# Attention and a mixture of experts on one core: where block one's last stores are issued, and where the first sums of w2 stand

## The chip, the cores and the metric

The kernel runs on one core of one Trainium2 chip. The metric is the device time of one execution in microseconds (us), the median of several runs. The core has five engines that work on their own: TensorE (PE, matrix multiplication), VectorE (DVE), ScalarE (ACT), GpSimd (POOL) and SyncE (SP), which here only issues DMAs. Each engine takes its instructions in the order in which the program wrote them, so an instruction that waits holds up all that stand behind it on that engine. That holds for the DMA issues too: those of SP stand in one line, and those of GpSimd stand in line with its arithmetic.

## The reference

```
attention (4 batches, 8 heads, 576 positions, width 64, 128 features):
  phi(x) = exp(x omT - |x|^2/2 - rowmax) / sqrt(128)
  out = (phi(q) (phi(k)^T v)) / (phi(q) sum(phi(k)) + 1e-6)
x = out as rows: 2304 x 512
mixture (4 experts, hidden width 1024):
  p = probs / (sum(probs) + 1e-9)
  y = sum over e of p[:, e] * (relu(x @ w1[e]) @ w2[e])
```

All is float32. The kernel reaches that precision with three matrix products for one: each operand is split into a high part (rounded to the matrix type) and a low part (what is left), and high*high, high*low and low*high are summed.

## The kernel before, in words

The mixture is done in 27 visits. A visit takes one half of one expert's hidden width (four chunks of 128) and one block of rows: visits 0 to 10 take block zero, 11 to 18 block one (768 rows, 6 output tiles of 128), 19 to 26 block two (1024 rows, 8 tiles). Visits of block one and two are in `fast` (L827). The first layer there is a seven-product scheme on quarter blocks (Strassen's), for two groups g of hidden chunks: `p1`, `p2`, `p5`, `p6`, `p7`, `p3`, `p4` are its products, each six matmuls of 512 columns in block two (L866). A product either opens a PSUM bank ("u", "b2", "b5") or, with start=False, adds onto one whose old contents were taken out before: `keep` (L870) copies a bank to SBUF on ScalarE, `both` (L876) adds a bank to such a copy on VectorE, after which ScalarE makes the relu's high part `hh` (L887) and VectorE its low part `hl` (L891). So p7(0) and p4(0) can start only when the bank "u" was read: p7(0) after the copy that p6(0) makes, p4(0) after the add that follows p7(0).

Visits of block two (`DEEP`, L475) use the same scheme for the second layer as well (`sevens`, L943), and for that they need sums of blocks of w2. The generator `w2_sides` (L540) makes them in steps: `sums_of(f)` is four tensor_tensor of 128x256 on GpSimd (L551 to L554) that read two loaded chunks of w2; `summed` splits half of such a sum (ScalarE copies the high part, GpSimd subtracts: line L498 and L501, tile w2s); `plain(c)` splits a chunk itself the same way (w2h, w2l); and a `load("w2")` behind plain(0), plain(2) and the second sums_of issues the load of a chunk on SP when a buffer is free (tile w2r, three buffers). For visit 19 the order of its steps is: sums 0, two splits of them, plain 0 with the load of its last chunk (called load (19,3) below), plain 1, plain 2 with a load, plain 3, sums 1 with two loads, two splits. `start_sides2` (L817) does the first step, `on_sides2` (L823) one further step, `prepare` (L848) as many as the list `steps2` says. At the head of visit 19 two steps are taken (L840), then one behind p1(0), one behind p5(0), one behind sum2(0), p2(1) and p7(0) each.

The split first layer of a block-two visit is not made again: `keep_sides` (L599) wrote it to DRAM in block one (eight DMAs on SP, `kept`), and `fetched` (L639) brings it back with eight DMAs that GpSimd issues (w1ah, w1al, w1sh, w1sl for two groups), two for each `next(ready)`. They wait until the buffers that they fill are free.

The output tiles of a visit: `outputs` (L684) multiplies, `gather` (L701) adds the result to the tile's accumulator on VectorE (L718), `gathered` (L725) counts; in the last visit of a block the finished accumulator is put on the list `stores`, and `store(keep)` (L733) issues stores on SP until `keep` are left. In visit 18 VectorE also makes the operands of block two between the gathers, steps of `build(2)` (L778): the differences `less` (L790) and the low parts xbl (L501) of seven 128x1024 tiles, two steps a tile.

Of the kernel before, what the change touches and what calls it, by code (L numbers as in the profile page):

```python
# [14 lines left out]
def attention_moe(ctx, tc, kT, qT, kd, qd, kn, qn, vn, omT, probs, w1, w2, out):  # L15
# [15 lines left out]
    E, FP, P, _ = w1.shape  # L31
# [34 lines left out]
    def bank(name):  # L66
        return psum.tile([P, 512], F32, tag="ps", name=name)
# [396 lines left out]
    def visit(u, n, c0, m):  # L464
        return (u, *HALVES[n], c0, m)

    BIG = {1: (START, 6 * P), 2: (START + 6 * P, 8 * P)}
    visits = [visit(0, n, 0, 2 * P) for n in range(3)]
# [6 lines left out]
    DEEP = range(N0 + NV, len(visits))  # L475
# [56 lines left out]
    def split_w2():  # L532
        if not later_w2:
            return
        v, c = later_w2.pop(0)
        W[v, "w2", c] = a, b = pair_of(("w2h", 512), ("w2l", 512))
        split(raw.pop((v, "w2", c)), a, b, nc.scalar, nc.gpsimd)
        load("w2")
# [145 lines left out]
    def outputs(v, hs, ps, t, cs):  # L684

        ts_ = slice(t * P, (t + 1) * P)
        for c in cs:
            (ha, hc), (wa, wc) = hs[c], W[v, "w2", c]
            nc.tensor.matmul(ps, ha[:, ts_], wa, start=(c == 0), stop=False)  # L689
            nc.tensor.matmul(ps, ha[:, ts_], wc, start=False, stop=False)  # L690
            nc.tensor.matmul(ps, hc[:, ts_], wa, start=False, stop=(c == FH - 1))  # L691
# [9 lines left out]
    def gather(v, ps, t, cs=slice(0, DM)):  # L701
        _, e, _, c0, n = visits[v]
        i = c0 // P + t
        sc = pr[:, i, e:e + 1]
        if i not in acc:
            if v in DEEP and t == 3:
                acc[i] = [att.tile([P, H], F32, tag=x, name="acc", bufs=1) for x in ("kvh", "kvl")]
            else:
                acc[i] = held([P, DM], "acc", F32)
        to = part(i, cs)  # L710
        fresh = [h for h in (0, H) if cs.start <= h < cs.stop and (i, h) not in begun_at]
        begun_at.update((i, h) for h in fresh)
        if fresh and v in DEEP:
            nc.vector.tensor_scalar(to, ps, sc, None, ALU.mult)
        elif fresh:
            nc.scalar.activation(to, ps, AF.Copy, scale=sc)
        else:
            nc.vector.scalar_tensor_tensor(to, ps, sc, to, ALU.mult, ALU.add)  # L718
# [6 lines left out]
    def gathered(v, t):  # L725
        i = visits[v][3] // P + t
        n = visits[v][4]
        n_tiles[i] += 1
        if n_tiles[i] == NV and v + 1 < len(visits):
            stores.append((i, acc.pop(i)))  # L730
        store(1 if v + 1 < len(visits) and t + 1 < n // P else 0)

    def store(keep):  # L733
        while len(stores) > keep:
            i, t = stores.pop(0)
            nc.sync.dma_start(out[i * P:(i + 1) * P], t)

    def plain(v):
# [18 lines left out]
        for t in range(tiles):  # L757
            ps = bank("g2")
            outputs(v, hs, ps, t, range(2))
            if v == N0 - 2 and t in (0, 2):  # L760
                next(building)
            if last:
                next(building, None)
            yield 0.5
            outputs(v, hs, ps, t, range(2, FH))
            gather(v, ps, t)
            gathered(v, t)
            for _ in range(FH // tiles):
                split_w()
            next(ready, None)  # L770
            if last:
                next(building, None)
            yield 0.5
# [43 lines left out]
    def start_sides2(v):  # L817
        B = {}
        g = w2_sides(v, B)
        next(g)  # L820
        sides2[v] = B, g

    def on_sides2(v):  # L823
        if v in sides2:
            next(sides2[v][1])

    def fast(v):  # L827

        u, _, _, _, n = visits[v]
        tiles, n = n // P, n // 2  # L830
# [3 lines left out]
        ready = sides(v + 1) if v + 1 < len(visits) else iter(())  # L834
# [13 lines left out]
        def prepare():  # L848
            if deep:
                for _ in range(steps2.pop(0)):  # L850
                    next(ready2, None)
            else:
                split_w2()
# [4 lines left out]
        def product(g, p, where, start=True):  # L858
            if start:
                P_[g][where] = bank("g1")[:, :n]  # L860
            ps = P_[g][where]
            (wa, wc), (xa, xc) = W[v, "w1", g][p], X[p]
            for k in range(2):
                w = slice(k * P, (k + 1) * P)
                for a, x, at in ((wa, xa, 0), (wa, xc, 1), (wc, xa, 2)):
                    nc.tensor.matmul(  # L866
                        ps, a[:, w], x[:, k], start=(start and k + at == 0), stop=(k == 1 and at == 2), skip_group_check=not start
                    )

        def keep(g, where, name):  # L870
            P_[g][name] = t = held([P, 512], "sum", F32)[:, :n]
            nc.scalar.activation(t, P_[g][where], AF.Copy)  # L872
# [23 lines left out]
        def p1(g):  # L896
            product(g, 1, "u")
            keep(g, "u", "p1")
# [4 lines left out]
        def sum2(g):  # L903
            both(g, 0, 0, "b2", "p1", hold=g == 1)
# [5 lines left out]
        def p6(g):  # L910
            product(g, 6, "u", start=False)
            keep(g, "u", "u2")
# [19 lines left out]
        def begun(t):  # L932
            g2[t] = bank("g2")
            outputs(v, hs, g2[t], t, range(2))
# [8 lines left out]
        def sevens():  # L943
# [87 lines left out]
            for t in range(tiles):  # L1031
                gathered(v, t)
# [10 lines left out]
        p6(0)  # L1043
        if deep:
            prepare()
        p1(1)
        sum2(0)
        if deep:
# [16 lines left out]
        if deep:  # L1065
# [6 lines left out]
            yield from sevens()  # L1072
            return
        prepare()
        p6(1)
        next(ready, None)
        begun(0)
        p7(1)
        begun(1)
# [5 lines left out]
        for t in range(tiles):  # L1085
            if t in g2:
                outputs(v, hs, g2[t], t, range(2, FH))
            else:
                g2[t] = bank("g2")
                outputs(v, hs, g2[t], t, range(FH))  # L1090
            gather(v, g2[t], t)
            gathered(v, t)
            next(ready, None)
            for _ in range(2 if t < 4 else 1):
                next(more, None)
            if v + 1 == DEEP[0] and t == 1:
                start_sides2(v + 1)
            elif t > 2:
                on_sides2(v + 1) if t < 5 else None
            yield 1  # L1100
        for _ in more:
            pass
# [205 lines left out]
    def emit():  # L1308
        pairs, g1 = begin()
        later = [Halves(b, hp) for b in range(1, B) for hp in range(NP)]  # L1310
        windows = {
            0: (first_rest(pairs, opening(later[0])), 15 / 11),
            3: (later_ticks(later[:-NP], True), 76 / 45.4),
            N0: (chain(opening(later[-NP]), later_ticks(later[-NP:], False)), 54 / (NV * (BIG[1][1] // P + 1) * 0.8)),
        }
        ticks, n, done, per = iter(()), 0, 0.0, 0
        for v in range(len(visits)):
            if v in windows:
                for _ in ticks:
                    pass  # L1320
                ticks, per = windows[v]
                n, done = 0, 0.0
            for share in first_visit(g1) if v == 0 else fast(v) if v >= N0 else plain(v):
                done += share
                while n < done * per:
                    next(ticks, None)
                    n += 1
        store(0)
# [61 lines left out]
```

## Time and profile before

| | us |
|---|---|
| runs timed: median (lowest to highest of 3) | 899.49 (898.46 to 899.87) |
| the profiled execution: time | 898.98 |
| its span, first to last instruction | 897.2 |
| busy: PE, VectorE, ScalarE, GpSimd | 884.8, 596.9, 468.3, 564.0 |
| mean granted clock of TensorE, share of full speed | 0.996 |

The span is the time from the first to the last instruction of the profiled execution; the time has about 2 us around it. All places given below as times, such as 584.08, are us from the start of the span. A timeline row has start, duration, engine, line, operation, what it writes and reads, shapes and how many; in brackets the time for which the engine sat idle before it and what ended that. Matmuls overlap, so a matmul's duration is longer than the step from one start to the next.

### The profile page before, as it was taken

The numbers are of one execution on the slowest core, as the hardware profiler recorded it, in microseconds if no ns is written. First come the engines' busy times: TensorE is split into PE (matmuls) and PEld (weight loads), VectorE is DVE, ScalarE is ACT, GpSimd is POOL, SyncE is SP. The second block draws the span as 40 slices with busy tenths as digits, with TensorE's granted clock in tenths as the row PEclk, the third lists the DMA queues.
The fourth block names the chain that finished last, engine by engine and source line by source line (L and its number), as shares of the span: only waits on it lengthen the run. The fifth ranks groups of instructions, "written<-read, shape, count | busy, mean of one in ns | idle before, by whom it ended". The sixth has DMA issues, their size and how long they took to land.

```text
span 897.2 us, 14825 instructions
## 1 busy us (share of the span) xinstructions
PE 884.8 (99%) x5484; PEld 789.6 (88%) x5484; DVE 596.9 (67%) x1026; ACT 468.3 (52%) x1038; POOL 564.0 (63%) x494
## 2 busy tenths in 40 slices
PE   9999999999999999999999999799999999999998
PEld 9988888889888898988988989589889898998988
DVE  6764567666778547577676676865858485675847
ACT  5555676776774565464555536244443434344442
POOL 6656464655645454435444345589898988989874
PEclk9999999999999999999999999999999999999999
DMA  7564454444521855545455255724151443415132
GB/s 184 171 221 118 136 161 146 153 135 151 168 71 47 314 173 209 214 136 189 174 194 212 71 188 214 256 58 154 59 176 54 159 135 112 154 59 176 43 135 94
DMA packets 64552, 134.01 MB, mean 149 GB/s; under 512 B 10624, under 2 KB 21056, under 8 KB 64480
## 3 DMA queue, kind: packets, MB, share of 16 engines
q1 hardware_dynamic: 54512, 102.95, 35.0%
q0 software_dynamic: 9360, 29.82, 10.0%
q8 instruction: 43, 0.70, 0.3%
q10 hardware_dynamic: 608, 0.30, 0.1%
q14 instruction: 29, 0.24, 0.1%
HBM read 98.96 MB, written 34.08 MB: 148 GB/s over the span
## 4 chain that ended last, share of the span: by engine, by line
PE 86%; DVE 8%; issue 2%; ACT 2%; DMA 1%; POOL 1%; SPq 0%; POOLq 0%; ACTq 0%; DVEq 0%
PE g L866 25%; PE g L941 17%; PE g L689 7%; PE g L691 7%; PE g L690 7%; PE g L674 3%; PE g L676 3%; PE g L675 3%; PE kv L314 2%; DVE xbl L501 2%; PE k_ps L266 1%; PE q_ps L266 1%; DMA kept<-w1ah 1%; PE qt_ps L325 1%; PE k_ps L147 1%
## 5 line engine op out<-in xcount | busy, mean ns | idle before, releaser
L501 POOL TENSOR_TENSOR w2l<-w2r,w2h 128x512 fp32r<-128x512 f32 x93 | 120.9, 1305 | 91.2 <-ACT w2h L498 77.7
L718 DVE SCALAR_TENSOR_TENSOR acc<-g,pr,acc 128x256 f32<-128x256 f32 (+1 forms) x278 | 139.3, 541 | 31.9 <-PE g L691 21.9
L501 POOL TENSOR_TENSOR w1sl<-w1r,w1sh 128x512 fp32r<-128x512 f32 (+1 forms) x43 | 75.2, 1749 | 70.8 <-ACT w1sh L498 54.7
L689 PE MATMUL g<-w2h,hh 128*128 128x512 f32 x280 | 112.7, 402 | 0.4 <-ACT kp L296 0.2
L691 PE MATMUL g<-w2h,hl 128*128 128x512 f32 x280 | 109.8, 392 | 0.0
L690 PE MATMUL g<-w2l,hh 128*128 128x512 f32 x280 | 109.6, 391 | 0.0
L891 DVE SCALAR_TENSOR_TENSOR hl<-sum,hh 128x384 fp32r<-128x384 f32 (+1 forms) x64 | 45.2, 709 | 85.6 <-ACT hh L887 55.8
L878 DVE TENSOR_TENSOR sum<-g,sum 128x384 f32<-128x384 f32 (+1 forms) x96 | 59.4, 620 | 64.3 <-PE g L866 57.1
L866 PE MATMUL g<-xbh,w1sh 128*128 128x384 f32 (+1 forms) x256 | 93.9, 367 | 5.5 <-ACT sum L872 5.5
L866 PE MATMUL g<-xbl,w1sh 128*128 128x384 f32 (+1 forms) x256 | 93.5, 365 | 1.1 <-DVE xbl L501 1.1
L866 PE MATMUL g<-xbh,w1sl 128*128 128x384 f32 (+1 forms) x256 | 93.1, 363 | 0.0
L501 POOL TENSOR_TENSOR w1al<-w1r,w1ah 128x512 fp32r<-128x512 f32 (+1 forms) x45 | 51.5, 1159 | 51.6 <-ACT w1ah L498 38.8
L872 ACT ACTIVATE sum<-g 128x384 f32<-128x384 f32 (+1 forms) x96 | 50.3, 540 | 50.2 <-PE g L866 49.3
L498 ACT ACTIVATE w2h<-w2r 128x512 fp32r<-128x512 f32 x90 | 55.0, 627 | 38.8 <-DMA w2r<-in_w 33.2
L866 PE MATMUL g<-xbh,w1ah 128*128 128x384 f32 (+1 forms) x192 | 70.1, 365 | 0.0
L866 PE MATMUL g<-xbl,w1ah 128*128 128x384 f32 (+1 forms) x192 | 69.6, 362 | 0.0
L866 PE MATMUL g<-xbh,w1al 128*128 128x384 f32 (+1 forms) x192 | 69.5, 362 | 0.0
L691 PEld LDWEIGHTS g<-w2h,hl 128*128 128x128 f32 x280 | 52.5, 188 | 11.9 <-DVE hl L924 0.4
L689 PEld LDWEIGHTS g<-w2h,hh 128*128 128x128 f32 x280 | 52.7, 188 | 11.2 <-DVE sum L878 0.7
L690 PEld LDWEIGHTS g<-w2l,hh 128*128 128x128 f32 x280 | 52.7, 188 | 8.6
L866 PEld LDWEIGHTS g<-xbh,w1sh 128*128 128x128 f32 x256 | 48.5, 189 | 11.8 <-ACT sum L872 6.0
L887 ACT ACTIVATE hh<-sum 128x384 fp32r<-128x384 f32 (+1 forms) x64 | 35.1, 551 | 41.5 <-DVE sum L878 41.0
(212 smaller groups left out, 2442.3 us busy)
## 6 DMA issues: line engine op xcount, KB each, us to landing
w2r<-in_w SPq DMA_DIRECT2D x108, 256.0 KB, 2.9
w1r<-in_w SPq DMA_DIRECT2D x38, 512.0 KB, 3.6
kept<-w1sh SPq DMA_DIRECT2D x16, 512.0 KB, 4.8
kept<-w1sl SPq DMA_DIRECT2D x16, 512.0 KB, 5.3
w1sh<-kept POOLq DMA_DIRECT2D x16, 512.0 KB, 6.1
w1sl<-kept POOLq DMA_DIRECT2D x16, 512.0 KB, 6.8
kept<-w1ah SPq DMA_DIRECT2D x16, 384.0 KB, 4.3
kept<-w1al SPq DMA_DIRECT2D x16, 384.0 KB, 4.4
```

Of the source, the lines that this page charges most:

```text
L498: hi.activation(a, t, AF.Copy)
L501: lo.tensor_tensor(c, t, f32(a), ALU.subtract)
L689: nc.tensor.matmul(ps, ha[:, ts_], wa, start=(c == 0), stop=False)
L690: nc.tensor.matmul(ps, ha[:, ts_], wc, start=False, stop=False)
L691: nc.tensor.matmul(ps, hc[:, ts_], wa, start=False, stop=(c == FH - 1))
L718: nc.vector.scalar_tensor_tensor(to, ps, sc, to, ALU.mult, ALU.add)
L866: nc.tensor.matmul(ps, a[:, w], x[:, k], start=(start and k + at == 0), stop=(k == 1 and at == 2), skip_group_check=not start)
L872: nc.scalar.activation(t, P_[g][where], AF.Copy)
L878: nc.vector.tensor_tensor(t, P_[g][where], t, ALU.add)
L887: nc.scalar.activation(ha, t, AF.Relu)
L891: nc.vector.scalar_tensor_tensor(x, y, 0.0, f32(z), ALU.max, ALU.subtract)
L941: nc.tensor.matmul(to, x, w, start=(start and f + k == 0), stop=(f + k == 3), skip_group_check=not start)
```

## The change

Three edits, all at the border between visit 18 and visit 19.

1. `gathered` issues no stores in visit 18; the six stores of block one are issued in visit 19, behind p6(0).
2. The first step of visit 19's `w2_sides` (the four sums) is taken in visit 18 ahead of p6(1) instead of behind output tile 1, and the `next(ready)` that stood behind p6(1), with two of GpSimd's load issues, is left out there, so that each of the four pairs of issues comes one output tile later.
3. The two splits of these sums come in output tiles 0 and 1, ahead of that tile's load issues, instead of tiles 3 and 4.

```diff
@@ gathered
-        store(1 if v + 1 < len(visits) and t + 1 < n // P else 0)
+        if v + 1 != DEEP[0]:
+            store(1 if v + 1 < len(visits) and t + 1 < n // P else 0)
@@ fast
         p6(0)
         if deep:
             prepare()
+            if v == DEEP[0]:
+                store(0)
         p1(1)
@@
         prepare()
+        if v + 1 == DEEP[0]:
+            start_sides2(v + 1)
         p6(1)
-        next(ready, None)
+        if v + 1 != DEEP[0]:
+            next(ready, None)
         begun(0)
@@
             gathered(v, t)
+            if t < 2:
+                on_sides2(v + 1)
             next(ready, None)
             for _ in range(2 if t < 4 else 1):
                 next(more, None)
-            if v + 1 == DEEP[0] and t == 1:
-                start_sides2(v + 1)
-            elif t > 2:
-                on_sides2(v + 1) if t < 5 else None
             yield 1
```

## Rows read from the trace of the kernel before

**Rows 1.** The page, its part 1: busy time of each engine.

```profile
PE 884.8 (99%) x5484; PEld 789.6 (88%) x5484; DVE 596.9 (67%) x1026; ACT 468.3 (52%) x1038; POOL 564.0 (63%) x494
```

**Rows 2.** Waits of TensorE, whole span: us in total, times, longest.

```profile
PE g L866 <- ACT sum L872: 5.5, 1, 5.5
```

**Rows 3.** The chain that ended last, around 580: start, us, what.

```profile
579.02 0.67 DVE acc L718
...
579.71 0.33 SPq L736
...
580.14 2.69 DMA w2r<-in_w
...
583.45 0.59 ACT sum L872
```

**Rows 4.** Timeline of TensorE from 568 to 593.

```profile
568.76 0.39 PE L866 MATMUL g<-xbh,w1ah 128*128 128x512 f32 x1
...
572.84 0.39 PE L866 MATMUL g<-xbh,w1sh 128*128 128x512 f32 x1
574.36 0.50 PE L866 MATMUL g<-xbl,w1sh 128*128 128x512 f32 x1 [1.12 <-DVE xbl L501]
...
578.16 0.39 PE L866 MATMUL g<-xbh,w1al 128*128 128x512 f32 x1
584.08 0.80 PE L866 MATMUL g<-xbh,w1sh 128*128 128x512 f32 x1 [5.53 <-ACT sum L872]
...
589.83 0.39 PE L866 MATMUL g<-xbh,w1ah 128*128 128x512 f32 x1
...
592.55 0.28 PE L941 MATMUL g<-w2h,hh 128*128 128x256 f32 x1
```

**Rows 5.** Stretches: length, busy PE, PEld, DVE, ACT, POOL, granted clock, DMA, GB/s.

```profile
584.10:588.00 3.90, 3.90 (x11) 3.10 (x12) 2.24 (x3) 2.51 (x5) 3.74 (x5) 0.58 0.00 0
```

**Rows 6.** Timeline of VectorE from 555 to 589.

```profile
555.91 0.55 DVE L924 SCALAR_TENSOR_TENSOR hl<-g,hh 128x384 fp32r<-128x384 f32 x1
...
561.68 1.22 DVE L501 TENSOR_TENSOR xbl<-raw_x,xbh 128x1024 fp32r<-128x1024 f32 x1
...
565.16 1.79 DVE L501 TENSOR_TENSOR xbl<-t_k,xbh 128x1024 fp32r<-128x1024 f32 x1
566.88 7.43 DVE L501 TENSOR_TENSOR xbl<-t_q,xbh 128x1024 fp32r<-128x1024 f32 x1
...
579.61 0.68 DVE L878 TENSOR_TENSOR sum<-g,sum 128x512 f32<-128x512 f32 x1
585.06 1.08 DVE L891 SCALAR_TENSOR_TENSOR hl<-sum,hh 128x512 fp32r<-128x512 f32 x1 [4.78 <-ACT hh L887]
...
588.04 0.68 DVE L878 TENSOR_TENSOR sum<-g,sum 128x512 f32<-128x512 f32 x1
```

**Rows 7.** Timeline of GpSimd from 552 to 574.

```profile
552.64 0.59 POOL L642 DMA_DIRECT2D w1ah<-kept  x1 [1.88 <-DMA kept<-w1ah]
...
560.98 0.76 POOL L551 TENSOR_TENSOR va<-w2r 128x256 f32<-128x256 f32 x1
...
563.57 1.60 POOL L553 TENSOR_TENSOR va<-w2r,va 128x256 f32<-128x256 f32 x1
...
566.92 2.56 POOL L501 TENSOR_TENSOR w2s<-va,w2s 128x512 fp32r<-128x512 f32 x2
569.44 3.77 POOL L501 TENSOR_TENSOR w2l<-w2r,w2h 128x512 fp32r<-128x512 f32 x3
```

**Rows 8.** Timeline of SP's DMA issues from 544 to 580.

```profile
544.50 4.12 SPq L494 DMA_DIRECT2D w2r<-in_w  x3
...
558.86 21.18 SPq L736 DMA_DIRECT2D out<-acc  x6
```

**Rows 9.** DMAs issued from 557 to 558: KB each, us to landing.

```profile
w1ah<-kept POOLq DMA_DIRECT2D x1, 384.0 KB, 10.1
w2r<-in_w SPq DMA_DIRECT2D x1, 256.0 KB, 9.9
```

## The prediction

> **What bounds the kernel now.** The page first: TensorE is busy 99% of the span [rows 1], so 12.4 us (897.2 less 884.8) is all that its waits can give back, and matmuls that run slowly come on top. Then TensorE's waits, of which the longest by far is one of 5.5 us on ScalarE's copy of a bank [rows 2]. TensorE's timeline at the head of visit 19 [rows 4] has it ahead of p7(0) at 584.08, and a shorter one, 1.1 on VectorE, in p6(0) at 574.36. The chain [rows 3] tells what is behind the long one, read upwards from 583.45: ScalarE's copy that p7(0) needs stood behind the split plain(3), whose chunk landed 2.69 us after SP issued it at 580.14; SP was at the sixth store until then, and that store waited for the last gather (579.02 to 579.69). The issue rows agree: the stores hold SP from 558.86 to 580.04 [rows 8]. The gather was late because VectorE was: one xbl took 7.43 us from 566.88, where another took 1.22 [rows 6], and it ended at 574.31, 1.1 us after GpSimd had come to the end (573.21) of five splits without a gap [rows 7]. That xbl is what p6(0) waited for too.
>
> What the two waits cost TensorE. Three products, 18 matmuls, step from 568.76 to 572.84: 0.2267 us each. The 36 matmuls of p1(0), p2(0), p5(0), p6(0), p1(1), p2(1) would end at 568.76 + 36 x 0.2267 = 576.92; they ended at 578.16 + 0.23 = 578.39 [rows 4]: 1.47 lost. From there to 584.08: 5.69 lost. The 30 matmuls of p7(0), p5(1), p3(0), p4(0), p6(1) took 584.08 to 592.55, 8.47 for 6.80: 1.67 lost, because the granted clock was 0.58 after the wait [rows 5], that is the lower level of 1.2 GHz for most of that stretch. Sum 8.83 us. After the wait of 1.1 us the clock did not suffer: the 17 matmuls from 574.36 to 578.39 took 4.03 for 3.85.
>
> **The change part by part.**
> *Stores behind p6(0).* SP now comes to load (19,3) as soon as its buffer is free, which is behind GpSimd's part of plain(0). That split ended at 570.7 (first of the three from 569.44, [rows 7]) and can't come much earlier, because its target is read by visit 18's last output tile, which ends at 568.76 [rows 4]. Issued at 569 to 570.7 and landing 2.7 later [rows 3], the chunk is there at 571.7 to 573.4. ScalarE wants it behind its copy of p5(0), whose matmuls end at 572.84 + 0.2: no wait. The copy of p6(0) is then done by about 575.5, and p7(0) starts when TensorE gets to it: 576.92. The six stores issue back to back at some 0.33 us each on an idle queue when the gathers are done; behind them on SP stand only the two loads of sums 1, for visit 20, whose sums come behind the split of T1, over 10 us later. Cost of that: 0. The accumulators are written again only by gathers that stand behind p7(1), p3(1), p4(1) and 48 matmuls of the second layer after L941's first (592.55 before), so nothing waits for the stores.
>
> *Sums ahead of p6(1).* The chunks they read are the second and third of three loads issued from 544.50 to 548.6 [rows 8], and GpSimd stood idle for 1.88 us before 552.64 [rows 7]. So the sums start about 551.3, 2.7 behind the last issue. They took 4.9 us at 560.98 to 565.9 against VectorE's xbl (1.60 for the third, 0.76 for the first, [rows 7]); I take 3.5 to 5. What they may hold up is VectorE in visit 18's p3(1) and p4(1): its last low part ends at 556.46 [rows 6]. The matmul that reads it is the 12th behind p4(1), and p4(1) ends 60 matmuls ahead of 568.76, at 555.16; so it is due at 555.16 + 11 x 0.2267 = 557.65, 1.2 later. If VectorE were kept out for all four sums, that is up to 4.9 less 1.2 = 3.7 us; if it goes in between, as in rows 7 beside xbl, nothing. I take 0: VectorE's instructions there are 0.55 long with idle time between. A gain isn't excluded here, it is counted below (VectorE's xbl).
>
> *Splits in tiles 0 and 1, load issues a tile later.* ScalarE gets to the first split behind the relu whose low part VectorE makes at 555.91 [rows 6], so GpSimd splits at about 556.4, and the first pair of fetches, at 552.64 before, is issued at 557.7; the second split at 558.8, the last pair of fetches by about 563.5 (before: up to 566.9, where the first split begins [rows 7]). p1(0) reads the first pair at 568.76, 11 us later; the slowest fetch took 10.1 [rows 9], while fetches, `kept` writes and stores were all in flight; now the stores are not. p5(0) reads the second pair at 571.5 (issued about 560.7), p1(1) the third at 574.2. Cost 0, with 1 us of cover by the slowest row and 4 or more by a quieter queue.
>
> *VectorE's xbl.* GpSimd now has, while VectorE works through its 16 instructions from visit 18's first gather to the add behind p2(0) (579.61 + 0.68 = 580.29, [rows 6]), two lone splits at 556.4 and 558.8, and plain(0) and plain(1) together, then plain(2) and plain(3) one by one, each behind a ScalarE copy. The excess before was 6.2 in the long xbl, 0.6 in the one ahead of it, and an estimated 0.4 in the difference ahead of that, 7.2. So the add ends between 573.1 (no excess) and 580.3 (the same). Six splits of 1.28 make 7.7 at most; I take two thirds, 5.1: the add ends at 578.2.
>
> The Trainium skill (SBUF — State Buffer, Who interferes with whom, and the section SBUF: two separate sides) has it that a VectorE instruction with two SBUF inputs and a GpSimd instruction that reads SBUF lock each other out, and that the one that starts first holds the port for its whole instruction. Read so, an xbl would wait out one split, not five, and 7.43 should have been about 2.5; rows 6 and 7 show otherwise for splits without a gap. By the rule the add would end at about 577 and the time would be near 890.5.
>
> *The new wait.* p4(0) adds onto the bank "u" that VectorE reads behind p7(0). From the add behind p2(0) VectorE and ScalarE need: relu 0.65, then from the hl at 585.06 to the end of the third add at 588.72 [rows 6] 3.66: together 4.3. Before, this was covered, since p4(0) came at 589.83. Now TensorE is ready for p4(0) at 576.92 + 18 x 0.2267 = 581.0, and the bank at 578.2 + 4.3 = 582.5 plus 0.1 for the hand-over. TensorE waits 1.6.
>
> **Sum.** 8.83 less 1.6 is 7.2. On the profiled execution's time: 898.98 - 7.2 = 891.8 us. That execution is 0.5 under the median of the runs shown (899.49), from which the same sum gives 892.3; both are within one another's spread.
>
> **The rivals.**
> - *VectorE is on time.* The add ends by 576.7, p4(0) waits for nothing: 898.98 - 8.83 = 890.2. For it: GpSimd has only two splits in a row now. Against: six splits fall into VectorE's work, and three lost turns of 1.28 on top of 573.1 make it late.
> - *VectorE is held as long as before.* If sums 1, now directly behind plain(3), keep it out again, the add ends at 580.3 or a little later; p4(0) waits 3.7 or more, with matmuls at the lower clock behind it (up to 1.67): 8.83 - 3.7 - 0 to 1.7 is 3.4 to 5.1, so 893.9 to 895.6. For it: the 7.43 row. Against: sums left VectorE its turn in rows 7.
> - *The load is late anyway, so the change doesn't do what it says.* Load (19,3) now shares the DMA engines with the last fetches, and the load issued among them took 9.9 [rows 9]. Then the chunk lands at 579 to 580.6, p7(0) starts at 580.2 to 581.8 instead of 576.9: 3.3 to 4.9 lost, and up to 1.67 to the clock. 892.3 to 896.7, say 894.5. Against: the fetches are issued by 563.5, six us before.
> - *Slower: the first fetches come too late.* The place is p1(0) at 568.76. It needs the sums, the split and two issues to go before on GpSimd. With the slowest load (9.9) ahead of the sums and the slowest fetch (10.1) behind, the sums start at 558.2, the pair is issued at about 563.8 and 564.9 and lands by 575; the second pair lands about 577.6, and TensorE is at 592.55 - 1 to 3, still not later than before. It decides when the second pair lands past 580.5, 12 us after p1(0)'s place less the 3 us of p1(0) and p2(0): then nothing of the 8.83 is left, and a clock drop puts it at 900 to 904. The fetches would have to take 13 us or more, which no row shows.
>
> **How the numbers follow.** Forecast 0.47 (891.8, by itself 890.6 to 893.4); VectorE on time 0.25; held as before 0.13; load late 0.07; sums in the way of visit 18's relus, 0 to 3.7 us off the forecast, 0.03 (893 to 895.5); slower 0.05. The range goes from 889.9, the whole 8.83 and 0.3 for the spread between runs, to 895.5, and leaves out the slower case and the far ends of two others. A time within 0.2% of before (1.8 us) can't be told from no change by these runs. Faster 0.93, same 0.03 (897.7 to 901.3: the ends of the two late cases and the near end of the slower one), slower 0.04.
>
> **What would show it.** In the profile after: SP's load of w2r at 569 to 571 and the six stores together at 574 to 580; no DMA on the chain around 580; TensorE's 5.5 us wait on ScalarE's sum gone, and in its place a wait of p4(0) on VectorE's sum (L878) of 1 to 2 us; granted clock 1.00 in all stretches of visit 19; GpSimd's sums at 551 to 556 and first fetch at 557 to 558; L941 begun at 584 to 586 instead of 592.55, and everything behind it shifted by the same amount. I am wrong if p1(0) waits for a fetch, if p7(0) still waits for ScalarE, or if what is gained at L941 is lost again later in visits 19 or 20.

## The result and the profile after

The changed kernel takes 891.5 us (median of 4 runs, 889.17 to 892.62); the kernel before, in runs beside it, 899.68. The ratio is 0.9905, 95% interval 0.9878 to 0.9932: faster by about 8 us, 0.9%. Run again later it took 891.49 (6 runs; ratio 0.9910, 0.9894 to 0.9925). Forecast were 891.8 and a range from 889.9 to 895.5, so the number was right. Its make-up was not quite: the border between the two visits gave back all of the 8.8 us, not 7.2, as the rival with VectorE on time had it.

TensorE's waits over the whole span of the profiled execution (total us, times, longest); this answers to [rows 2]:

```profile
PE warm L1120 <- DVE om_r L1111: 1.1, 1, 1.1
PE k_ps L147 <- DVE om L82: 0.8, 1, 0.8
PE g L942 <- DVE hl L925: 0.7, 2, 0.5
PE g L689 <- ACT kp L296: 0.2, 1, 0.2
```

The wait of 5.5 us and the one of 1.1 on xbl are gone, and none has come in their place: the two longest are at the start of the program. TensorE's timeline at the head of visit 19, first matmuls of p1(0), p4(0) and the second layer (lines have moved by one), answers to [rows 4]:

```profile
570.97 0.39 PE L867 MATMUL g<-xbh,w1ah 128*128 128x512 f32 x1
...
583.21 0.40 PE L867 MATMUL g<-xbh,w1ah 128*128 128x512 f32 x1
...
585.94 0.28 PE L942 MATMUL g<-w2h,hh 128*128 128x256 f32 x1
```

From p1(0) to the second layer are 585.94 - 570.97 = 14.97 us for 66 matmuls, 0.2268 each; before it was 592.55 - 568.76 = 23.79 [rows 4]. That is 8.82 gained in this stretch. The granted clock in it was 1.00 (window row: length, busy PE, PEld, DVE, ACT, POOL, clock, DMA, GB/s), where [rows 5] had 0.58:

```profile
570.97:585.94 14.97, 14.97 (x68) 12.38 (x66) 12.41 (x14) 7.72 (x14) 12.67 (x10) 1.00 0.68 231
```

SP's issues, answering to [rows 8]:

```profile
571.61 0.33 SPq L494 DMA_DIRECT2D w2r<-in_w  x1
```

```profile
576.50 3.68 SPq L737 DMA_DIRECT2D out<-acc  x6
```

Load (19,3) goes out at 571.61, 0.6 after p1(0) began, instead of 11.4 after, and lands 3.8 later; the six stores hold SP for 3.7 us instead of 21.2. VectorE and GpSimd, answering to [rows 6, 7]:

```profile
571.01 3.89 DVE L501 TENSOR_TENSOR xbl<-raw_x,xbh 128x1024 fp32r<-128x1024 f32 x2
574.83 0.74 DVE L718 SCALAR_TENSOR_TENSOR acc<-g,pr,acc 128x512 f32<-128x512 f32 x1
575.49 1.65 DVE L501 TENSOR_TENSOR xbl<-raw_x,xbh 128x1024 fp32r<-128x1024 f32 x1
577.06 0.74 DVE L718 SCALAR_TENSOR_TENSOR acc<-g,pr,acc 128x512 f32<-128x512 f32 x1
577.72 0.68 DVE L879 TENSOR_TENSOR sum<-g,sum 128x512 f32<-128x512 f32 x1
...
582.27 0.68 DVE L879 TENSOR_TENSOR sum<-g,sum 128x512 f32<-128x512 f32 x1
```

```profile
560.90 0.59 POOL L642 DMA_DIRECT2D w1ah<-kept  x1
...
569.84 6.21 POOL L501 TENSOR_TENSOR w2l<-w2r,w2h 128x512 fp32r<-128x512 f32 x3 [2.47 <-ACT w2h L498]
```

No xbl takes 7.43 any more; two side by side take 3.89. Three of GpSimd's splits take 6.21, where three took 3.77 before [rows 7]: now GpSimd loses turns too. The add behind p2(0) ends at 578.40, 7.4 after p1(0) began, against 11.5 before; the add that p4(0) needs ends at 582.95, and p4(0) starts at 583.21, just when the 54 matmuls ahead of it are through (570.97 + 54 x 0.2268 = 583.22). Its margin is 0.26 us, and 0.26 in the repeat too (584.29 and 584.55). The first fetch went out at 560.90, 10.1 ahead of p1(0), and nothing waited for it. How long the first pair took to land (KB, us from issue to landing):

```profile
w1ah<-kept POOLq DMA_DIRECT2D x1, 384.0 KB, 5.6
w1al<-kept POOLq DMA_DIRECT2D x1, 384.0 KB, 6.0
```

So w1ah was there at 566.5 and w1al at 567.5, some 4.4 and 3.9 us ahead of the matmuls that read them (570.97 and 571.42).

Behind this stretch nothing changed: from the second layer's first matmul to the last matmul of the kernel are 301.04 us before and 301.28 after. Ahead of it this execution was 2.2 us late, and that has nothing to do with the change. 2.07 of the 2.21 are there at TensorE's first L266 matmul, in the attention, some 470 us ahead of the first edited step (before, then after):

```profile
82.11 1.16 PE L266 MATMUL k_ps<-om_r,k 64*128 64x128 f32 x16
```

```profile
84.18 1.16 PE L266 MATMUL k_ps<-om_r,k 64*128 64x128 f32 x16
```

8.82 less 2.21 less 0.24 is 6.4, the difference of the two spans (897.2 and 890.8).

### The profile page after: what moved, and what is told of

Read it like the earlier page. It is cut to its first block, busy times and chain, and to the rows that moved or that the text cites. A ratio compares the mean times of both kernels' runs of the same rounds, so it can differ in the third digit from the quotient of the medians.

```text
span 890.8 us, 14823 instructions
## 1 busy us (share of the span) xinstructions
PE 884.1 (99%) x5484; PEld 789.4 (89%) x5484; DVE 593.8 (67%) x1026; ACT 468.9 (53%) x1038; POOL 566.3 (64%) x494
## 4 chain that ended last, share of the span: by engine, by line
PE 90%; DVE 4%; issue 2%; DMA 2%; ACT 1%; POOL 1%; SPq 0%; POOLq 0%; ACTq 0%; DVEq 0%
PE g L867 26%; PE g L942 17%; PE g L689 8%; PE g L691 7%; PE g L690 7%; PE g L674 3%; PE g L676 3%; PE g L675 3%; PE kv L314 2%; PE q_ps L266 1%; PE k_ps L266 1%; DMA kept<-w1ah 1%; PE qt_ps L325 1%; PE k_ps L147 1%; PE q_ps L147 1%
## 5 line engine op out<-in xcount | busy, mean ns | idle before, releaser
L501 POOL TENSOR_TENSOR w2l<-w2r,w2h 128x512 fp32r<-128x512 f32 x93 | 123.9, 1337 | 81.6 <-ACT w2h L498 69.8
```

What stands on the lines that cost most here:

```text
L501: lo.tensor_tensor(c, t, f32(a), ALU.subtract)
```

## The experiments

All stretches below run from p1(0)'s first matmul to the first of the second layer in visit 19, in each kernel's profiled execution; without any wait it is 14.97. "Lost to the clock" is the time of the matmuls behind a wait, up to the end of the stretch, less 0.2268 for each. Each ratio is to runs of the kernel before made beside that kernel: their medians were 899.68 for "changed", 899.95 for "changed again", the two halves and the first "splits in tiles 3, 4", and 899.6 for the rest.

| kernel | stretch | wait at | lost to the clock | median us (runs) | ratio, interval |
|---|---|---|---|---|---|
| before | 23.79 | p6(0) 1.47 in all, p7(0) 5.7 | 1.7 | 899.6 (25) | |
| changed | 14.97 | none | 0 | 891.5 (4) | 0.9905, 0.9878 to 0.9932 |
| changed again | 15.02 | none | 0 | 891.49 (6) | 0.9910, 0.9894 to 0.9925 |
| stores only | 21.28 | p6(0) 1.7 in all, p4(0) 2.9 | 1.7 | 897.01 (8) | 0.9968, 0.9955 to 0.9981 |
| sums and splits only | 19.92 | p7(0) 3.2 | 1.75 | 895.23 (6) | 0.9951, 0.9935 to 0.9968 |
| splits in tiles 3, 4 | 17.21 | p4(0) 2.1 | 0.1 | 891.76 (5) | 0.9907, 0.9892 to 0.9923 |
| the same again | 15.61 | p4(0) 0.5 | 0.1 | 892.98 (6) | 0.9931, 0.9908 to 0.9954 |
| VectorE two more | 20.67 | p4(0) 3.1 | 2.6 | 895.74 (6) | 0.9958, 0.9938 to 0.9978 |
| VectorE five more | 24.69 | p4(0) 8.2 | 1.6 | 901.03 (10) | 1.0011, 0.9997 to 1.0025 |
| fetches late | 18.10 (23.89 from where p1(0) is due) | p1(0) 5.8 | 3.1, a second wait in it | 899.82 (10) | 1.0003, 0.9988 to 1.0018 |

**Stores alone** (edit 1 on the kernel before).

```diff
 gathered:
-        store(1 if v + 1 < len(visits) and t + 1 < n // P else 0)
+        if v + 1 != DEEP[0]:
+            store(1 if v + 1 < len(visits) and t + 1 < n // P else 0)
 fast, behind p6(0) and prepare():
+            if v == DEEP[0]:
+                store(0)
```

> The kernel before with edit 1 alone: the six stores behind p6(0) of visit 19, sums and splits where they were. Theory A (two causes: SP's stores ahead of load (19,3), and GpSimd's five splits in a row that keep VectorE's xbl out): the 5.5 us wait of p7(0) goes, the 1.1 us wait of p6(0) on xbl stays, and p4(0) now waits for VectorE about 2.3 us, because the add behind p2(0) still ends 11.5 us after p1(0) begins, as before. From p1(0)'s first matmul to the first of L942: 23.8 - 8.8 + 1.5 + 2.3 = 18.8 us; time about 895. Theory B (the stores alone are the whole gain): 15.0 to 16.4 us, time 890 to 892.

Measured: stretch 21.28, 897.01 us, 2.9 below the runs of before beside it (899.95). TensorE's rows show which waits remain:

```profile
574.62 0.50 PE L867 MATMUL g<-xbl,w1sh 128*128 128x512 f32 x1 [1.34 <-DVE xbl L501]
...
585.64 0.53 PE L867 MATMUL g<-xbh,w1ah 128*128 128x512 f32 x1 [2.75 <-DVE sum L879]
...
590.09 0.28 PE L942 MATMUL g<-w2h,hh 128*128 128x256 f32 x1
```

The wait of p7(0) is gone, that of p6(0) stays, and p4(0) waits for VectorE, as theory A had it; B (the stores are the whole gain) is out. A's size was short by 2.5 us (21.28 for 18.8), for two reasons, and the time, expected at about 895, came out 2 us above. VectorE's and GpSimd's rows:

```profile
567.14 7.43 DVE L501 TENSOR_TENSOR xbl<-t_q,xbh 128x1024 fp32r<-128x1024 f32 x1
574.49 0.74 DVE L718 SCALAR_TENSOR_TENSOR acc<-g,pr,acc 128x512 f32<-128x512 f32 x1
575.15 3.40 DVE L501 TENSOR_TENSOR xbl<-raw_x,xbh 128x1024 fp32r<-128x1024 f32 x2
```

```profile
575.74 1.73 POOL L551 TENSOR_TENSOR w2f<-w2r 128x256 f32<-128x256 f32 x1
577.54 1.60 POOL L552 TENSOR_TENSOR w2f<-w2f,w2r 128x256 f32<-128x256 f32 x1
```

The xbl is 7.43 us long to the hundredth again. The second reason is the clock, below; the first is VectorE. Now that the load is early, the second sums of w2 follow at once and meet VectorE's last xbl (two in 3.40, sums of 1.73 and 1.60 where 0.74 is usual), so the add behind p2(0) ends 12.8 after p1(0), not 11.5. And the wait of 2.75 was followed by the lower clock:

```profile
585.60:589.50 3.90, 3.86 (x10) 3.06 (x11) 2.29 (x3) 1.26 (x3) 1.81 (x2) 0.56 0.00 0
```

**Sums and splits alone** (edits 2 and 3 on the kernel before).

```diff
 the changed kernel, with edit 1 taken out:
-        if v + 1 != DEEP[0]:
+        if True:
             store(1 if v + 1 < len(visits) and t + 1 < n // P else 0)
 ...
-            if v == DEEP[0]:
-                store(0)
```

> The kernel before with edits 2 and 3 alone: sums and splits early, the stores of block one in visit 18 as before. Theory A: xbl is no longer long, the last gather ends about 6.8 us after p1(0) begins instead of 10.9, the sixth store lets SP go 0.4 later, load (19,3) lands 2.7 after that, and p7(0), due 8.2 after p1(0), starts near 11.3 after a wait of 3 us on ScalarE; then 0 to 1.7 us are lost to the clock. From p1(0) to the second layer 18 to 19.7 us, time 894 to 896. Theory B (stores are the whole gain): as before, 23.8 us and 899.5.

Measured: stretch 19.92 and 895.23 us, 4.7 below before, in A's range (its stretch 0.2 above). VectorE was on time (the gather that the sixth store waits for ended 6.8 after p1(0) began), but SP still issued the load behind that store, and ScalarE's split of the chunk, with the copy that p7(0) needs behind it, waited for the DMA; the rows are VectorE's last gather, ScalarE's and TensorE's:

```profile
574.13 0.74 DVE L718 SCALAR_TENSOR_TENSOR acc<-g,pr,acc 128x512 f32<-128x512 f32 x1
```

```profile
578.26 0.63 ACT L498 ACTIVATE w2h<-w2r 128x512 fp32r<-128x512 f32 x1 [5.26 <-DMA w2r<-in_w]
```

```profile
579.43 0.51 PE L867 MATMUL g<-xbh,w1sh 128*128 128x512 f32 x1 [3.05 <-ACT sum L873]
```

So each half of the change leaves the other cause standing. By the stretches the halves give 2.5 and 3.9 alone and 8.8 together: each alone turns part of its gain into a wait that the other would remove, and both of those waits cost a clock drop on top.

**Splits in tiles 3 and 4** (edit 3 undone), run twice.

```diff
             gathered(v, t)
-            if t < 2:
-                on_sides2(v + 1)
             next(ready, None)
             for _ in range(2 if t < 4 else 1):
                 next(more, None)
+            if 2 < t < 5:
+                on_sides2(v + 1)
             yield 1
```

> The changed kernel with edit 3 undone: stores late, sums ahead of p6(1), but the two splits of the sums in tiles 3 and 4 as before. Theory A: two w2s and two or three w2l splits stand in a row on GpSimd again, one xbl is 5 us or longer, p6(0) waits 1 to 1.5 us for it and p4(0) 1 to 2.5: from p1(0) to the second layer 17.5 to 19 us, time 893.5 to 895.5. Rival (the lock falls free after each GpSimd instruction, so the order of the splits doesn't matter): 15.0 us, same time as the changed kernel.

> The changed kernel with the two splits in tiles 3 and 4 once more, since its trace showed a wait of 2.0 us at p4(0) which its median (891.76 beside 891.49) did not. If the wait is there in each execution: from p1(0) to the second layer 17 to 17.5 again, and a median 1 to 3 us above 891.5 once more runs are pooled. If it was one execution's: about 15.0 us and 891.5.

The first execution, TensorE, VectorE and GpSimd, then the second:

```profile
583.16 0.50 PE L867 MATMUL g<-xbh,w1ah 128*128 128x512 f32 x1 [1.96 <-DVE sum L879]
```

```profile
564.77 4.02 DVE L501 TENSOR_TENSOR xbl<-t_k,xbh 128x1024 fp32r<-128x1024 f32 x1
568.71 2.31 DVE L501 TENSOR_TENSOR xbl<-t_q,xbh 128x1024 fp32r<-128x1024 f32 x1
```

```profile
565.14 2.56 POOL L501 TENSOR_TENSOR w2s<-va,w2s 128x512 fp32r<-128x512 f32 x2
567.67 8.98 POOL L501 TENSOR_TENSOR w2l<-w2r,w2h 128x512 fp32r<-128x512 f32 x4
```

```profile
581.36 0.50 PE L867 MATMUL g<-xbh,w1ah 128*128 128x512 f32 x1 [0.36 <-DVE sum L879]
```

```profile
564.57 1.99 DVE L501 TENSOR_TENSOR xbl<-t_k,xbh 128x1024 fp32r<-128x1024 f32 x1
566.47 2.31 DVE L501 TENSOR_TENSOR xbl<-t_q,xbh 128x1024 fp32r<-128x1024 f32 x1
```

```profile
565.68 2.02 POOL L501 TENSOR_TENSOR w2s<-va,w2s 128x512 fp32r<-128x512 f32 x1 [0.22 <-ACT w2s L498]
```

Neither theory holds as written. In the first, an xbl was held 2.8 us through two splits, and p4(0) waited; in the second GpSimd paused 0.22 us between the two, waiting for ScalarE, VectorE got its turn, and little was left of the wait. A row of splits without a gap is not enough to keep VectorE out: the four that follow in the first execution took 8.98 us, 2.2 each, and three xbl of VectorE ended among them. No execution had an xbl of 5 us, and p6(0) waited in neither. The 11 times lie between 889.91 and 896.52 with a median of 892.1, the ten of the changed kernel between 889.17 and 893.62 with 891.5. So edit 3 is worth between 0.6 and 2.2 us by the two traces and 0.6 by the medians, which these runs can't tell from nothing. What takes p6(0)'s wait away is there without edit 3, then; of edit 2's two parts, the earlier sums and the later load issues, no run has one alone.

**What VectorE may lose.** The changed kernel with the last xbl of visit 18 written again, two or five times.

```diff
         for p, t in ((5, t1), (6, t2), (7, b12), (3, b22), (4, b21)):
             halve(p, t)
+            if u == 2 and p == 4:
+                for _ in range(2):      # or 5
+                    nc.vector.tensor_tensor(X[p][1], t, f32(X[p][0]), ALU.subtract)
             yield
```

> The changed kernel, with the last xbl of visit 18 written three times instead of once by VectorE (two more 128x1024 subtractions, 1.1 us each alone, ahead of the last gather; the result is the same). Theory C (p4(0) waits for VectorE's add behind p7(0), and in the changed kernel that add ends 0.26 us before p4(0) is due): the add comes 2.2 us or more later, p4(0) waits 2.0 to 3, from p1(0) to the second layer 17 to 18, or up to 19.7 if the clock falls; time 893.5 to 896. Rival (the add is not what sets p4(0), or VectorE has slack there): 15.0 us, time as the changed kernel.

> The same with five more subtractions: 5.7 us or more on VectorE. Theory C: p4(0) waits 5.4 to 7 and the matmuls behind it lose about 1.7 to the lower clock; from p1(0) to the second layer 22 to 24, time 898.5 to 900.5, that is all of the gain given back. Rival: 15.0 us, or a part of the 5.7.

The extra subtractions (L816) with two and with five, p4(0) in the first and in the second, and the first one's clock behind it:

```profile
575.16 3.88 DVE L816 TENSOR_TENSOR xbl<-raw_x,xbh 128x1024 fp32r<-128x1024 f32 x2
```

```profile
574.61 8.90 DVE L816 TENSOR_TENSOR xbl<-raw_x,xbh 128x1024 fp32r<-128x1024 f32 x5
```

```profile
584.34 0.79 PE L870 MATMUL g<-xbh,w1ah 128*128 128x512 f32 x1 [2.98 <-DVE sum L882]
```

```profile
588.80 0.80 PE L870 MATMUL g<-xbh,w1ah 128*128 128x512 f32 x1 [8.01 <-DVE sum L882]
```

```profile
584.34:588.20 3.86, 3.86 (x9) 3.08 (x10) 2.21 (x2) 1.04 (x3) 1.77 (x2) 0.50 0.00 0
```

Theory C holds: p4(0) hangs on VectorE's add, with next to no slack in the changed kernel. p4(0) came 4.05 and 4.04 us after the end of the add behind p2(0), the prediction's 4.4 being nearly right (in the changed kernel, where one of these VectorE instructions takes 1.19 instead of 0.69 beside GpSimd's sums, the add that p4(0) needs ends 4.55 after). The sizes were low: the two extra subtractions took 3.88 and the five 8.90, 1.8 to 1.9 each instead of 1.1, while GpSimd's second sums, 1.6 to 1.7 each, ran beside them; with two, the clock cost 0.4 us more behind the stretch. Both stretches, 20.67 and 24.69, lie above what was expected (up to 19.7 and up to 24). With five, all of the gain was given back: 901.03, expected up to 900.5.

**The price of the slower rival.** The changed kernel with the fetches at the head of visit 19.

```diff
+    held_back = {}
 ... fast:
+        late = held_back.pop(v, ())
         ready = sides(v + 1) if v + 1 < len(visits) else iter(())
+        if v + 1 == DEEP[0]:
+            held_back[v + 1] = ready
 ... at the head of visit 19:
                 for _ in range(2):
                     on_sides2(v)
+                for _ in late:
+                    pass
 ... output tiles:
-            next(ready, None)
+            if v + 1 != DEEP[0]:
+                next(ready, None)
```

> The changed kernel, with all eight fetches of visit 19's first-layer weights issued by GpSimd at the head of visit 19, behind the splits plain 0 and 1, instead of in output tiles 0 to 3. It measures the price of the slower rival: GpSimd ends plain 1 some 3 us after p1(0) is due, the first pair lands 4 to 5 us after that on an idle DMA queue. p1(0) waits 6 to 8 us, matmuls behind it lose about 1.7 to the clock, while VectorE and ScalarE catch up, so nothing else waits: time 898 to 901. If the fetches have less to them than that (landing in 2 to 3 us): 895 to 897.

GpSimd's first fetch, the time to landing of the first pair, TensorE's p1(0), and two windows behind it:

```profile
572.53 0.59 POOL L642 DMA_DIRECT2D w1ah<-kept  x1
```

```profile
w1ah<-kept POOLq DMA_DIRECT2D x1, 384.0 KB, 3.1
w1al<-kept POOLq DMA_DIRECT2D x1, 384.0 KB, 3.9
```

```profile
575.75 0.77 PE L873 MATMUL g<-xbh,w1ah 128*128 128x512 f32 x1 [5.79 <-DMA w1ah<-kept]
```

```profile
575.75:579.30 3.55, 3.40 (x7) 2.29 (x8) 0.37 (x1) 0.04 (x1) 1.10 (x3) 0.50 0.92 274
579.30:585.00 5.70, 5.70 (x21) 4.55 (x20) 0.69 (x1) 2.60 (x5) 1.84 (x2) 0.79 1.12 407
```

899.82 us, as expected, and no different from before (ratio 1.0003): fetches 12.6 us later than in the changed kernel, counted from where p1(0) is due (569.96 here, 570.97 there), undo the gain to the last us. The wait was 5.8 and not 6 to 8: p1(0) begins with w1ah, which landed 3.1 after its issue, and not with the pair, whose w1al landed at 577.0, 4.5 after the first issue, and held up p1(0)'s third matmul. That second wait, about half a us, is in the 3.1 of the table; the rest is the clock, expected at 1.7. The 3.1 us of an idle queue do not give the margin of the changed kernel, where the DMA queues were busy and the first pair took 5.6 and 6.0 to land: what it has to spare there is 4.4 and 3.9 us.

## Why the prediction came out as it did

*What bounds the kernel, and the 8.83.* Right, and shown by parts: stores alone took away p7(0)'s wait and left p6(0)'s; sums and splits alone did the reverse; both together left 14.97 us, the 66 matmuls without a gap. The slow matmuls behind the long wait went with it, as counted.

*Stores behind p6(0).* Right. The load was issued 0.6 us into p1(0), in the forecast span (0.2 to 1.9 after p1(0) is due). It landed 3.8 later, not 2.7, while the last fetches were still in flight (till 574.7; with the stores alone the last landed 0.6 us after the load's issue, and it took 2.7); ScalarE did not wait. The rival "load late anyway" (9.9) did not come; the lower end of its time doesn't follow from its own terms either, which give 893.4 (898.98 - 8.83 + 3.3) and not 892.3. The six stores cost nothing.

*Sums ahead of p6(1).* Cost 0, as forecast. They ran from 553.36 to 556.74 here (551.2 to 554.5 if the 2.2 us late start is taken off), and TensorE has no wait in visit 18.

*Load issues a tile later.* Cost 0, as forecast; the smallest margin was 3.9 us, more than the 1 us that rows 9 allowed and near the 4 of the prediction. But the queue was hardly quieter: from 560 to 570 the DMAs moved 340 GB/s on the mean, against 386 from 555 to 560 before.

*VectorE's xbl, the step that was mis-sized.* I took 5.1 us of excess for VectorE between its first gather in visit 18 and the add behind p2(0), two thirds of six splits. It was 3.1: this part lasted 18.11 us (560.29 to 578.40) against 22.20 before with its 7.2. Two splits in three were counted as time that VectorE loses; the rows after show GpSimd losing turns as well (three splits in 6.21 for 3.8). The rival with VectorE on time stood at 0.25 and is what happened. By the Trainium skill (SBUF — State Buffer, Who interferes with whom), which was weighed there, whichever of the two engines issues first holds the other off for one whole instruction. The estimate made by that rule was an add near 577, 8.2 after p1(0); it ended 7.4 after. In this kernel the rule was the better guide than the 7.43 row; in the one before and with the stores alone it was not, since there VectorE's instruction starts first in the trace (566.88 against the split's 566.92, 567.14 against 567.19) and was held through five splits.

*The new wait.* The wait of 1.6 us that the forecast put at p4(0) did not come, because of that size. The dependence exists, but is not reached: p4(0) needs the add, which came 0.26 us early. The 1.6 of the forecast came from the 2.0 us that the excess was too large. VectorE's extra subtractions and the stores-only kernel show the wait itself.

*Why 891.5 and not 890.2, then?* The stretch gave 8.82, the medians differ by 8.1 (899.6 and 891.5), and the interval of the second run, 6.7 to 9.5 us, holds 8.8. The profiled executions show what scatters: one was 2.1 us late by 84 us into the span, and the repeat 3.5 late by p1(0), with a TensorE wait of 2.4 on ScalarE near 324 that the other executions don't have. Both lie in code that the change does not touch. So that the median came within 0.3 of the forecast is partly luck: the forecast's 1.6 of wait and the scatter ahead of the border cancel. Of the executions without a trace no run shows where their time went.

## What to carry to other kernels

A DMA issue that waits for a late engine holds every load behind it on its queue, as the six stores held load (19,3) for over 9 us here: put stores of finished results behind the loads that the next stage needs, and count each as a wait of the queue's whole line. Where two causes end in one wait, undo them one by one: each alone left over half of the joint gain in the other's wait. After such a change look for the next engine's margin (here 0.26 us on VectorE's add), since that is what the next edit will hit.

## What the runs showed of the hardware that was not expected

The price of a TensorE wait is not its length. Behind waits of 0.4, 1.1, 1.3 and 2.0 us the granted clock stayed at 1.00 and at most 0.2 us were lost; behind 2.75, 2.98, 3.05, 5.5, 5.8 and 8.0 us it was 0.50 to 0.58 in the next 3.5 to 3.9 us (1.2 GHz, the lower level, for most of it), and the matmuls of the stretch lost 1.7, 2.6, 1.75, 1.7, 3.1 (some 0.5 of it a second wait) and 1.6, not in the order of the waits.

Which of VectorE and GpSimd goes first when both have work queued is not settled by these runs. An xbl stood through five of GpSimd's splits in a row in two kernels (7.43 both times), through two in another (4.02), and took turns one by one in the rest, where GpSimd's splits took up to 2.3 us each instead of 1.28. What decides it was not tried. In the two cases of 7.43 VectorE's instruction and GpSimd's first split began within 0.05 us of each other, in the third 0.37 us apart; in all three VectorE's began first, and it was the one that was held.
